# A new opening order for a chunked state-space scan and a GELU expert on one core: decay rows in one load, constants moved, half of a mask off VectorE

## The chip, the cores and the metric

The kernel runs on one core of a Trainium2 chip. The metric is the device time of one execution in microseconds, as the median of several runs. A core has TensorE (PE, with its weight loads PEld), VectorE (DVE), ScalarE (ACT), GpSimd (POOL) and SyncE (SP), which here only issues transfers; ACT's queue issues a few as well.

## The reference

Two stages, computed in one kernel. The first is a chunked linear recurrence over 4 batches, 8 heads, 768 positions, with 32 values and 16 state entries for each head:

```
log_a = log(clip(a, 1e-6, 1))
for each chunk c:
    cum  = cumsum(log_a of the chunk)
    L    = exp(cum_i - cum_j), lower triangle only
    y    = ((C B^T) * L) x  +  (C state) * exp(cum)
    state = exp(sum of log_a) * state + sum_j B_j x_j exp(cum_last - cum_j)
```

The second takes y as 3072 tokens of 256 values: `out = gelu_tanh(y @ w_in) @ w_out` with w_in of 256x2048 and w_out of 2048x256. Everything comes and goes in float32; the kernel works in bfloat16 inside.

## The kernel before

The 768 positions of a batch are cut into 6 chunks of 128; two chunks of a batch are a unit u (0 to 11), so a unit is 256 tokens. Units 0 to 2 belong to batch 0, 3 to 5 to batch 1, and so on. The work is a list of named steps, made by `add(engine, function, ...)`. The order in which they are issued, and so the order on every engine and every queue, is written out by hand in the string `ORDERED` (L19 to L72). `name.u.i:E` is a step with its arguments and, where there is a choice, its engine (A for ACT, D for DVE, P for POOL, S for SP). `~n` is a fill: matmuls of zeros on PE over n times 128 columns, written to a bank that nobody reads (L693). A step waits only for what it depends on, but each engine takes its own steps strictly in this order.

The steps that matter here:

- The decay of batch 0's first four chunks. `load_aq` brings the rows (four loads of 16 KB, L158), `clipq` clips them, `Rq` scans them (products from the end of a chunk), `tpq` turns them to positions on partitions, `recip0` takes the reciprocal (L335 to L348). `peq`, `ppq` and `pendq` make the decay of a whole chunk for each head: a small product on DVE, a matmul with the selection matrix `selp` on PE, a copy (L350 to L360). The decay of all other chunks goes the same way through `load_a`, `clip`, `R`, `tp2`, `tp6`, `recip1`, `recip`, `pe`, `pp`, `pend`.
- `mulb` and `mulc` scale B and C by decay and inverse decay, `tw` turns them on PE, `ew` copies the turned blocks out of PSUM (L408 to L431).
- `G.u` multiplies B and C of a unit into banks ga and gb (L591). `M.u.0` and `M.u.1` (DVE, L604) mask ga and gb with the triangle `tri`. For unit 0 the second half goes another way: `GE` copies a bank of gb out on ACT (L609), and `ME` masks the copy on POOL by a select, or on DVE by a product (L612).
- x of the first four chunks is loaded in one piece of 512 KB (`load_x4`), cast in two halves of its heads (`x4.0`, `x4.1`, L551), and brought into chunk order on PE by `XX.u` with the matrix `unp` that `c_unp` builds (L256); `xn` copies it out. `XD.u` is the state's new part.
- `S.c` carries the state on (DVE), `SP.c` spreads it by head under `bmask` for the next chunk (L681). `Y.u` sums the masked part and the state's part (L634), `yev.u` copies it to `xm`, the expert's input.
- The expert: `s1.u.i` (i = 0 to 7) is four matmuls into one of two banks hp (L700), `gelu.u.i` takes the bank to bfloat16 on ACT (L712), `s2.c.q` is four matmuls that add a quarter of the second product of chunk c (L717), `oev.c` copies the sum out and `store.c` stores it.
- The weights come as four pieces of w_in (`load_wi.q`) and four of w_out (`load_wo.q`), 512 KB each, and are cast in halves (`wi.q.k`, `wo.q.k`). `s1.u.i` needs piece i/2 (rounded down) of w_in, `s2.c.q` needs piece q of w_out.
- Constants: `c_ident`, `c_tri`, `c_bmask`, `c_m8`, `c_cz` are made on POOL, `c_zero`, `c_m4`, `c_sel` (a reduction, and the copy that makes `selp`), `c_par`, `c_unp` on DVE. `c_warm` runs the GELU once on one value.

Of the kernel before, what the change touches and what calls it, by code (L numbers as in the profile page):

```python
# [17 lines left out]
SCR = (2, 3)  # L18
ORDERED = """  # L19
# [8 lines left out]
gelu.0.3 load_bc.1.0 s1.0.4 wi.3.0:A s1.0.5 gelu.0.4 Y.1 tp2 mul1.0 gelu.0.5 yev.1.0.2:A s1.0.6  # L28
s1.0.7 gelu.0.6 load_x.2 tp6.0 load_bc.1.1 load_x.3 gelu.0.7 recip1 T1.0 s2.0.1.0.o s1.1.0 bh1:D N1
s1.1.1 wo.1.1:A tp6.3 s2.0.0.1.o wo.2.1:P gelu.1.0 gelu.1.1 mul1.1 tp6.2 T1.1 tp6.1 ce1.1:A ce1.0:A  # L30
wo.2.0:A bn1:D recip.1.4 s2.0.1.1.o s1.1.2 s1.1.3 gelu.1.2 wo.3.0:A wo.3.1:P G.2 gelu.1.3 s2.0.0.2.o
s2.0.1.2.o s2.0.0.3.o castx.2.None:P s2.0.1.3.o load_bc.2.1 M.2.0 mul.1.0 M.2.1 oev.1:A s1.1.4
s1.1.5 T.1.0 load_x.4 oev.0:A s2.1.0.0.o castx.3.None:P s2.1.0.1.o gelu.1.4 SP.3 D.2 gelu.1.5 s1.1.6
S.2.0 SP.4 load_x.5 E.1.0:A N.1 mul.1.1 bn.1:D gelu.1.6 s1.1.7 Y.2 s2.1.0.2.o T.1.1 gelu.1.7
yev.2.0.2:A s1.2.0 s1.2.1 gelu.2.0 E.1.1:D F.1 s2.1.0.3.o s1.2.2 gelu.2.1 gelu.2.2 D.3 load_bc.2.0
oev.2:D G.3 S.3.0 S.3.1 s2.1.1.0.o load_x.6 castx.4.None:P s1.2.3 gelu.2.3 s2.1.1.1.o s2.1.1.2.o
# [51 lines left out]
def kernel(  # L88
# [53 lines left out]
    def a_rows(t, n):  # L142
        return bass.AP(tensor=a.tensor, offset=a.offset + t, ap=[[S, batch * H], [1, n]])
# [112 lines left out]
    def c_unp():  # L256
# [3 lines left out]
        for r in range(R4):  # L260
            nc.vector.tensor_copy(out=unp[:, r, :, r], in_=sub)
# [701 lines left out]
```

## Time and profile before

| | |
|---|---|
| device time, median of 2 runs | 117.23 us (117.01 to 117.46) |
| span of the profiled execution | 115.1 us |
| its granted TensorE clock | 1.000 |
| PE busy | 109.4 us (95%) |
| ACT busy | 75.1 us (65%) |
| DVE busy | 68.7 us (60%) |
| POOL busy | 15.1 us (13%) |

The page gives for the profiled execution the span from its first to its last instruction, and no other time of its own; the device times of the two runs also hold what lies around that span. PE's busy time counts the fills, and its ends are modelled. Busy shares are averages: the first 14 us, the next 15 and the rest have different limits, and are read apart. A row of the timeline has the start and the busy time in us, then the engine and the line; where like instructions are merged (x2, x14) the busy time is that of all of them.

### The profile page before, as it was taken

What the parts mean: (1) busy time and instruction counts of PE and PEld (TensorE: products, weight loads), DVE (VectorE), ACT (ScalarE), POOL (GpSimd) and SP (SyncE); (2) the same over time, 40 slices, a digit from 0 to 9 for tenths busy, and PEclk for the clock granted to TensorE, in tenths of its full rate; (3) what the DMA queues carried; (4) which work ended last, traced back from release to release, by engine and by line L of the source; (5) the groups of instructions that cost most, each with busy time, mean ns of one, the idle gap of its engine ahead of it and who ended that gap; (6) DMA issues with size and microseconds to landing.
All of it is one profiled execution on the core that took longest, in us unless ns stands there. A gap on an engine that the chain in (4) does not pass through costs nothing.

```text
span 115.1 us, 3372 instructions
## 1 busy us (share of the span) xinstructions
PE 109.4 (95%) x1425; PEld 92.2 (80%) x1425; DVE 68.7 (60%) x135; ACT 75.1 (65%) x149; POOL 15.1 (13%) x32
## 2 busy tenths in 40 slices
PE   6999799999999999999999999999999999999990
PEld 2354578978877979799898998998989989999970
DVE  6688799998799989196966281546827421000100
ACT  3119889978657767657576486377766765685710
POOL 6564274122220000020002000000000000000000
PEclk9999999999999999999999999999999999999999
DMA  2999999949969828959478760000014014001132
GB/s 65 236 280 286 397 293 311 278 84 218 225 109 226 214 64 203 192 147 265 102 158 184 174 178 0 6 0 0 0 50 138 0 49 139 0 0 51 46 103 79
DMA packets 43006, 15.97 MB, mean 139 GB/s; under 512 B 36656, under 2 KB 41456, under 8 KB 42992
## 3 DMA queue, kind: packets, MB, share of 16 engines
q1 hardware_dynamic: 42848, 15.68, 53.9%
q8 instruction: 11, 0.18, 0.6%
q10 hardware_dynamic: 144, 0.08, 0.4%
q14 instruction: 3, 0.02, 0.1%
HBM read 11.04 MB, written 3.93 MB: 130 GB/s over the span
## 4 chain that ended last, share of the span: by engine, by line
PE 82%; DMA 8%; SPq 4%; POOL 1%; issue 1%; ACT 0%
PE hp L709 36%; PE o_ps L727 33%; DMA wf<-in_moe_w_out_dram 8%; PE yb L727 3%; PE ga L595 3%; PE yb L650 2%; PE yb L659 2%; SPq L190 1%; PE hp L628 1%; SPq L162 1%; SPq L159 1%; SPq L150 1%; POOL w_out_sb L316 1%; POOL w_in_sb L316 1%; SPq L183 1%
## 5 line engine op out<-in xcount | busy, mean ns | idle before, releaser
L713 ACT ACTIVATE gT<-hp 128x512 bf16<-128x512 f32 x96 | 53.3, 595 | 24.5 <-PE hp L709 24.0
L709 PE MATMUL hp<-xm,w_in_sb 128*128 128x256 bf16 x384 | 51.9, 273 | 0.5 <-ACT pend L314 0.3
L727 PE MATMUL o_ps<-w_out_sb,gT 128*128 128x256 bf16 x352 | 46.4, 273 | 0.0
L709 PEld LDWEIGHTS <-w_in_sb 128*128 128x128 bf16 x384 | 41.2, 114 | 3.2 <-issue 1.7
L727 PEld LDWEIGHTS <-gT 128*128 128x128 bf16 x384 | 37.0, 98 | 4.7 <-issue 0.8
L318 DVE COPY o_sb<-o_ps 128x256 f32<-128x256 f32 x7 | 3.0, 424 | 22.4 <-PE o_ps L727 18.4
L605 DVE TENSOR_TENSOR m<-ga,tri 128x1024 bf16<-128x1024 f32 x12 | 14.6, 1216 | 0.0
L605 DVE TENSOR_TENSOR m<-gb,tri 128x1024 bf16<-128x1024 f32 x11 | 13.4, 1219 | 0.5 <-PE gb L595 0.5
L697 PE MATMUL yb<-wz 128*128 128x512 bf16 (+2 forms) x24 | 8.2, 491 | 1.1 <-DVE warm L222 1.1
L314 ACT ACTIVATE o_sb<-o_ps 128x256 f32<-128x256 f32 x15 | 5.6, 382 | 4.1 <-PE o_ps L727 3.0
L683 DVE SCALAR_TENSOR_TENSOR sp_new<-s_new,pend,bmask 128x256 bf16<-128x256 f32 x17 | 8.0, 479 | 0.1
L316 POOL CAST x<-x_t 128x512 bf16<-128x512 f32 x5 | 3.2, 648 | 34.9 <-DMA x_t<-in_x_dram 22.9
L676 DVE SCALAR_TENSOR_TENSOR s_new<-s_new,pend,hp 128x64 f32<-128x64 f32 x13 | 3.6, 279 | 5.7 <-PE hp L628 5.5
L697 PEld LDWEIGHTS <-wz 128*128 128x128 bf16 x25 | 2.9, 126 | 5.0 <-issue 3.6
L659 PE MATMUL yb<-m,x 128*32 128x128 bf16 x192 | 6.1, 219 | 0.0
L650 PE MATMUL yb<-ce,sp_new 128*32 128x128 bf16 x160 | 5.3, 220 | 0.0
L595 PE MATMUL ga<-ce,bh 32*128 32x256 bf16 x48 | 4.7, 272 | 0.1
L314 ACT ACTIVATE xm<-yb 128x512 bf16<-128x512 f32 x8 | 4.8, 597 | 0.0
L595 PE MATMUL gb<-ce,bh 32*128 32x256 bf16 x48 | 4.7, 273 | 0.0
L727 PE MATMUL yb<-w_out_sb,gT 128*128 128x256 bf16 x32 | 4.1, 273 | 0.0
L659 PEld LDWEIGHTS <-x 128*32 128x32 bf16 x192 | 3.8, 97 | 0.4 <-issue 0.2
L650 PEld LDWEIGHTS <-sp_new 128*32 128x32 bf16 x160 | 3.0, 96 | 1.0 <-issue 1.0
(108 smaller groups left out, 78.4 us busy)
## 6 DMA issues: line engine op xcount, KB each, us to landing
out_dram<-o_sb SPq DMA_DIRECT2D x24, 128.0 KB, 2.0
x_t<-in_x_dram SPq DMA_DIRECT2D x20, 128.0 KB, 3.8
wf<-in_moe_w_in_dram SPq DMA_DIRECT2D x4, 512.0 KB, 8.3
wf<-in_moe_w_out_dram SPq DMA_DIRECT2D x4, 512.0 KB, 8.9
bc_t<-in_B_dram SPq DMA_DIRECT2D x3, 384.0 KB, 4.8
bc_t<-in_C_dram SPq DMA_DIRECT2D x3, 384.0 KB, 4.3
scr<-bc SPq DMA_DIRECT2D x4, 192.0 KB, 3.1
x_t<-in_x_dram SPq DMA_DIRECT2D x1, 512.0 KB, 4.8
```

The costliest lines, as they stand in the source:

```text
L314: nc.scalar.activation(o, i, AF.Copy)
L316: nc.gpsimd.tensor_copy(out=o, in_=i)
L595: nc.tensor.matmul(out=gbank(g)[:, 256 * k:256 * k + 256], lhsT=bh_of(2 * u + k)[gs], rhs=ce_of(2 * u + k)[gs], start=True, stop=True, til ...
L605: nc.vector.tensor_tensor(out=m_of(u)[:, 2 * i:2 * i + 2].rearrange("p g k e t -> p (g k e) t"), in0=gx[i].rearrange("p g (k t) -> p (g k) ...
L650: nc.tensor.matmul(out=y4[32 * j:32 * j + 32, k, w], lhsT=sp[:, 32 * h:32 * h + 32], rhs=ce_of(gc)[:, h % 2], start=first(j), stop=False, ...
L659: nc.tensor.matmul(out=y4[32 * j:32 * j + 32, k, w], lhsT=X16[u][:, k, 32 * h:32 * h + 32], rhs=m[:, h // 2, h % 2, :], start=first(j), st ...
L676: nc.vector.scalar_tensor_tensor(out=s_new, in0=state[("s", gc - 1)], scalar=pend_of(gc), in1=d, op0=ALU.mult, op1=ALU.add)
L683: nc.vector.scalar_tensor_tensor(out=sp_new.rearrange("p (g d) -> p g d", g=4), in0=(XN[0][:, H * D:H * D + 64] if gc == 0 else state[("s" ...
L697: nc.tensor.matmul(out=t[:, 0:m * 128], lhsT=wz, rhs=w3.to_broadcast([128, m, 128]), start=True, stop=True, skip_group_check=True)
L709: nc.tensor.matmul(out=hp[:, j * T:(j + 1) * T], lhsT=w_in_k[:, w, q, k], rhs=xm[:, w, u * T:(u + 1) * T], start=(w == 0), stop=(w == 1))
L713: nc.scalar.activation(gts[u][:, 2 * i:2 * i + 2], hps.pop((u, i)).rearrange("p (j t) -> p j t", j=2), AF.Gelu_apprx_tanh)
L727: nc.tensor.matmul(out=ops[gc], lhsT=gts[u][:, fi, k * Q:(k + 1) * Q], rhs=w_out_sb[:, fi, :], start=(fi == 0 and (u > 0 or k == 0)), stop ...
```

## The change

- `load_aq` is one load of 128 rows of 512 B on ACT's queue (the rows that are not used hold shifted decays), in place of four on two queues.
- `c_unp` becomes two steps: the zeros on POOL (`c_unp0`), and one copy with four diagonals in place of four copies. `c_m4` moves ahead of `c_zero`; `c_bmask`, `c_cz`, `c_tri` come right behind `c_ident`; `c_par` and `c_sel` stand between `tpq` and `peq`; `c_m8` comes much later.
- x of the first four chunks is loaded and cast by unit: `x4.u.k` handles 64 partitions, so `XX.0` needs only the first half of the partitions. That makes four casts.
- Unit 1's gb goes the way of unit 0's: `GE.1.2` and `GE.1.3` on ACT, `ME.1.2` on POOL, `ME.1.3` on DVE (it has a buffer of its own).
- `SP.c` may run on POOL for every chunk but the first, as two instructions with a float32 tile between them. The new order does so for chunks 1, 2, 3, 6, 7 and 10; the others stay on DVE.
- `load_bc0` brings B ahead of C; `load_wo.0` comes right behind `load_wi.0`; B of the last two chunks of batch 0 and of batch 1 come ahead of `load_wi.2`, C of batch 1 ahead of `load_wi.3`.
- A first s1 step no longer waits for the last one of the unit before (unit 1 only), and the whole order is new: units 0 and 1 go through the expert in turns, unit 3 is handled ahead of unit 2.

```diff
-c_wz c_ident c_zero c_unp load_aq.2:A load_bc0.1 c_tri load_aq.1:S load_aq.3:S load_aq.0:A c_m8
-c_sel c_warm c_m4 load_bc0.0 load_x4 clipq Rq tpq load_a.0:A load_a.1:S peq ~53 ppq pendq:A
-load_wi.0 c_cz c_bmask recip0 mulc.0:D mulc.1:D mulb:P ~9 tw.1 tw.0 ew.0.0:D c_par ew.0.1:A tw.2
-ew.0.2:A x4.1:D ~8 G.0 clip ew.1.0:A ew.1.1:A load_wi.1 M.0.0 GE.3 x4.0:P GE.2 load_wi.2 ~2 XX.0
-XD.0 load_wo.0 xn.0:A ew.1.2:A SP.0 S.0.0 xn.1:A wi.0.0:A wi.0.1:A R ~13 G.1 S.0.1 load_wi.3 XX.1
-load_bc1.0 xn.2:A ME.3:P ME.2:P pe Y.0 XD.1 pp yev.0.0.2:A S.1.0 load_wo.1 load_bc1.1 SP.1 S.1.1
-load_wo.2 wi.1.1:P M.1.0 wi.2.0:P wo.0.0:D pend:A wo.0.1:P wi.2.1:P SP.2 wi.1.0:A M.1.1 s1.0.0
-gelu.0.0 s1.0.1 gelu.0.1 xn.3:A wi.3.1:P s1.0.2+4 gelu.0.2 s1.0.3 s2.0.0.0.o load_wo.3 wo.1.0:P
...
+c_wz load_aq:A load_bc0.0 load_bc0.1 c_ident c_cz c_bmask c_tri c_m4 c_zero clipq Rq tpq c_par c_sel
+peq mulb:P c_unp0 load_x4.0 load_x4.1 load_wi.0 ~33 ppq recip0 pendq:D tw.0 mulc.0:D c_warm ew.0.0:A
+load_a.0:A load_a.1:A load_wo.0 load_wi.1 mulc.1:P x4.0.0:P x4.0.1:P ~8 tw.1 ew.0.1:A tw.2 c_unp
+ew.1.0:D ew.0.2:A x4.1.1:P x4.1.0:D ~15 G.0 ew.1.1:A ew.1.2:A GE.0.3 M.0.0 XX.0 GE.0.2 ME.0.3:P XD.0
+xn.0:A xn.1:A S.0.0 ME.0.2:P ~4 G.1 SP.0 S.0.1 ~3 Y.0 XX.1 M.1.0 SP.1:P XD.1 wi.0.1:D load_bc1.0
+load_bc.1.0 load_wi.2 load_bc1.1 S.1.0 wi.0.0:P GE.1.3 GE.1.2 ME.1.2:P yev.0.0.2:A xn.2:A xn.3:A
+SP.2:P s1.0.0 ME.1.3:D Y.1 gelu.0.0 s1.0.1 c_m8 wo.0.0:P wi.1.0:P wo.0.1:P wi.1.1:P yev.1.0.2:A
+gelu.0.1 s1.1.0 s1.1.1 gelu.1.0 gelu.1.1 S.1.1 clip R pe tp2 mul1.0 tp6.3 tp6.0 recip1 tp6.1 tp6.2
+s2.0.0.0.o mul1.1 load_wo.1 pp s1.1.2 pend:A load_bc.1.1 s1.1.3 T1.0 s2.0.1.0.o gelu.1.2 load_wi.3
+gelu.1.3 s1.0.2 load_wo.2 bh1:A gelu.0.2 load_wo.3 load_x.3 mul.1.0 s1.0.3 gelu.0.3 wi.2.1:P
+wi.2.0:P N1 T1.1 s1.1.4 bn1:A s1.0.4 gelu.1.4 wo.1.1:P wo.1.0:P wi.3.0:P T.1.0 gelu.0.4 s1.0.5
+load_x.2 ce1.0:A recip.1.4 ce1.1:D s1.1.5 gelu.0.5 mul.1.1 s2.0.0.1.o gelu.1.5 E.1.0:D T.1.1
+s2.0.1.1.o E.1.1:A wi.3.1:D N.1 bn.1:A F.1 wo.2.1:P s1.0.6 s1.0.7 wo.2.0:D gelu.0.6 G.3 s2.0.0.2.o
+gelu.0.7 M.3.1 M.3.0 wo.3.1:A s2.0.1.2.o s1.1.6 load_x.4 gelu.1.6 wo.3.0:P s2.0.0.3.o s2.0.1.3.o
+s1.1.7 castx.3.None:P oev.0:A oev.1:D load_x.5 load_x.7 load_bc.2.1 D.3 S.3.0 SP.6:P castx.2.None:P
+SP.3:P gelu.1.7 G.2 s2.1.0.0.o s2.1.0.1.o s2.1.0.2.o M.2.0 M.2.1 s2.1.0.3.o D.2 Y.3 oev.2:A
...
-    def load_aq(i, eng):
-        (nc.scalar if eng == "ACT" else nc.sync).dma_start(out=aq_t[32 * i:32 * i + 32], in_=a_rows(i * Q, Q))
+    def load_aq(eng):
+        (nc.scalar if eng == "ACT" else nc.sync).dma_start(
+            out=aq_t, in_=bass.AP(tensor=a.tensor, offset=a.offset, ap=[[P4, 16], [S, H], [1, Q]]))
...
-    def load_x4():
-        nc.sync.dma_start(out=x4_t, in_=x[0, :, 0:R4 * Q, :].rearrange("h (p r) d -> p h (r d)", r=R4))
+    def load_x4(u):
+        nc.sync.dma_start(out=x4_t[64 * u:64 * u + 64], in_=x[0, :, u * T:(u + 1) * T, :]
+                          .rearrange("h (p r) d -> p h (r d)", r=R4))
...
-        nc.vector.memset(unp, 0.0)
+    def c_unp0():
+        nc.gpsimd.memset(unp, 0.0)
...
-        for r in range(R4):
-            nc.vector.tensor_copy(out=unp[:, r, :, r], in_=sub)
+        d = unp[:, 0, :, 0]
+        diag = bass.AP(tensor=d.tensor, offset=d.offset, ap=[list(d.ap[0]), [Q + 1, R4], [R4, P4]])
+        nc.vector.tensor_copy(out=diag, in_=sub.rearrange("p (o q) -> p o q", o=1).to_broadcast([128, R4, P4]))
...
-    def f_GE(g):
-        nc.scalar.activation(ge0[:, g - 2], gbank(g), AF.Copy)
+    def f_GE(u, g):
+        nc.scalar.activation(ge0[GEU.index(u)][:, g - 2], gbank(g), AF.Copy)
...
+        if eng == "POOL":
+            sc = spf[gc % 2]
+            nc.gpsimd.tensor_scalar(out=sc, in0=state[("s", gc)], scalar1=pend_of(gc + 1), scalar2=None, op0=ALU.mult)
+            nc.gpsimd.tensor_tensor(out=sp_new.rearrange("p (g d) -> p g d", g=4),
+                                    in0=sc.rearrange("p (o d) -> p o d", o=1).to_broadcast([128, 4, 64]),
+                                    in1=bmask.rearrange("p (g d) -> p g d", g=4), op=ALU.mult)
...
-        if u:
+        if u not in GEU:
...
-                s.deps.append(s1.get((u - 1, NI - 1)))
+                s.deps.append(s1.get((u - 1, NI - 1)) if u > 1 else None)
```

More of the change, by code (lines that the diff above doesn't have):

```diff
@@ L31 @@
[L31 to L36, printed above, removed]
@@ L72 @@
+s1.11.2 oev.20:A s1.11.3 store.20 gelu.11.2 s2.10.1.0.o store.18 gelu.11.3 s2.10.1.1.o s1.11.4
+s1.11.5 gelu.11.4 s2.10.1.2.o gelu.11.5 s2.11.0.0.yb s1.11.6 s1.11.7 gelu.11.6 s2.10.1.3.o gelu.11.7
+s2.11.0.1.yb oev.21:D s2.11.0.2.yb store.21 s2.11.0.3.yb s2.11.1.0.o oev.22:A s2.11.1.1.o store.22
+s2.11.1.2.o store.19 s2.11.1.3.o oev.23:A store.23
 """
@@ L156, in load_bc1 @@
                           .rearrange("h (p r) n -> p h (r n)", r=n))
-    def load_aq(i, eng):
-        (nc.scalar if eng == "ACT" else nc.sync).dma_start(out=aq_t[32 * i:32 * i + 32], in_=a_rows(i * Q, Q))
+    def load_aq(eng):
+        (nc.scalar if eng == "ACT" else nc.sync).dma_start(
+            out=aq_t, in_=bass.AP(tensor=a.tensor, offset=a.offset, ap=[[P4, 16], [S, H], [1, Q]]))
     def load_a(i, eng):
-        (nc.scalar if eng == "ACT" else nc.sync).dma_start(out=a_t[32 * i:32 * i + 32], in_=a_rows(i * HS, HS))
+        (nc.scalar if eng == "ACT" else nc.sync).dma_start(out=a_t[32 * i:32 * i + 32], in_=a_rows(i, HS))
     def load_bc(b, i):
@@ L297 @@
     xm = const.tile([128, 2, n_tokens], BF16, name="xm")
+    spf = [const.tile([128, 64], FP32, name=f"spf{i}") for i in range(2)]
     gx = [ps1.tile([128, 2, 512], FP32, name=f"g{i}") for i in "ab"]
@@ L549, with f_x4 @@
     XN = {}
[L551 to L553 removed]
+    def f_x4(u, k, eng):
+        ps, ks = slice(64 * u, 64 * u + 64), slice(4 * k, 4 * k + 4)
+        copy(eng, x4b[ps, ks].rearrange("p h r d -> p h (r d)"), x4_t[ps, ks])
     def f_XX(u):
@@ L679, in f_S, with f_SP @@
         state[("s", gc)] = s_new
-    def f_SP(gc):
+    def f_SP(gc, eng):
         sp_new = st.tile([128, 256], BF16, name="sp_new")
+        if eng == "POOL":
[4 more added lines that the diff above has]
+                                    in1=bmask.rearrange("p (g d) -> p g d", g=4), op=ALU.mult)
+            state[("sp", gc)] = sp_new
+            return
         nc.vector.scalar_tensor_tensor(
@@ L772 @@
     add("A", c_warm, deps=[cz0])
-    cunp = add("D", c_unp, deps=[cid])
+    cu0 = add("P", c_unp0)
+    cunp = add("D", c_unp, deps=[cid, cu0])
     cpar = add("D", c_par, deps=[cbm])
```

101 lines of the change are left out of this document (47 added, 54 removed).

## The prediction, made before the changed kernel had run

> **What bounds the kernel now.** I read the page first, then the table of four stretches, then the timeline of the opening and of the stretch behind it, then the chain and the transfers issue by issue.
>
> ```profile
> span 115.1 us, 3372 instructions
> ...
> PE   6999799999999999999999999999999999999990
> ...
> DMA  2999999949969828959478760000014014001132
> GB/s 65 236 280 286 397 293 311 278 84 218 225 109 226 214 64 203 192 147 265 102 158 184 174 178 0 6 0 0 0 50 138 0 49 139 0 0 51 46 103 79
> ...
> PE 82%; DMA 8%; SPq 4%; POOL 1%; issue 1%; ACT 0%
> ```
> ```profile
> 0.00:14.18 14.18, 12.01 (x161) 5.89 (x162) 10.48 (x36) 7.13 (x18) 7.27 (x20) 1.00 0.86 252
> 14.18:29.00 14.82, 14.32 (x167) 12.23 (x166) 14.16 (x27) 13.28 (x27) 5.24 (x8) 1.00 0.92 236
> 29.00:107.70 78.70, 78.70 (x1062) 70.30 (x1061) 43.65 (x73) 52.85 (x102) 2.62 (x4) 1.00 0.46 106
> ```
>
> The second table gives, behind each stretch, its length and the busy time of PE, PEld, DVE, ACT and POOL, the granted clock, the DMA share and GB/s. From 29 us on TensorE never stops, in either order of the same work, so I cost that stretch at nothing: what can move the time lies before it. Up to 14.18 PE's busy time is mostly fill matmuls, and between 14.18 and 29 DVE and ACT are nearly full too and the transfers run at 0.92. The question is thus when the first expert matmul (s1.0.0) starts and how tightly PE works until weights and units are all there.
>
> ```profile
> 0.80 0.91 ACTq L159 DMA_DIRECT2D aq_t<-in_a_dram  x2
> ...
> 1.05 5.76 PE L697 MATMUL yb<-wz 128*128 128x512 bf16 x14 [1.05 <-DVE warm L222]
> ...
> 1.75 0.28 DVE L258 TENSOR_REDUCE sub<-ident 128x32 bf16<-128x128 bf16 x1
> ...
> 3.67 0.45 POOL L238 TENSOR_SCALAR_AFFINE_SELECT bmask<-bmask 128x256 bf16<-128x256 bf16 x1
> 3.70 0.50 DVE L273 COPY selp<-sel 128x128 f32<-128x128 f32 x1
> ...
> 5.16 0.23 DVE L328 TENSOR_SCALAR acq<-aq_t 128x128 f32<-128x128 f32 x1 [0.89 <-DMA aq_t<-in_a_dram]
> ...
> 5.88 0.40 DVE L342 STREAM_TRANSPOSE rt<-rq_t 128x128 f32<-128x128 f32 x1
> ...
> 6.21 0.25 DVE L351 TENSOR_SCALAR peq<-m,acq,rq_t 128x4 f32<-128x4 f32 x1
> ...
> 6.37 1.05 POOL L416 TENSOR_TENSOR bc0s<-bcf,rt 128x512 bf16<-128x512 f32 x1 [1.74 <-DVE rt L342]
> ...
> 6.80 1.24 DVE L409 TENSOR_TENSOR cz<-bcf,pt 128x256 bf16<-128x256 f32 x2
> 6.85 0.65 PE L697 MATMUL yb<-wz 128*128 128x512 bf16 x3
> 7.03 0.17 ACT L314 ACTIVATE pendq<-hp 128x4 f32<-128x4 f32 x1 [3.79 <-PE hp L356]
> ...
> 8.76 0.21 DVE L266 TENSOR_REDUCE par<-bmask 128x1 f32<-128x4 bf16 x2
> ...
> 9.08 0.28 PE L595 MATMUL ga<-ce,bh 32*128 32x256 bf16 x2
> ...
> 9.51 1.23 DVE L605 TENSOR_TENSOR m<-ga,tri 128x1024 bf16<-128x1024 f32 x1
> ...
> 10.22 1.22 POOL L616 TENSOR_SCALAR_AFFINE_SELECT m<-ge 128x512 bf16<-128x512 bf16 x2 [1.71 <-ACT ge L610]
> ...
> 11.07 0.48 DVE L683 SCALAR_TENSOR_TENSOR sp_new<-o_ps,pendq,bmask 128x256 bf16<-128x256 f32 x1 [0.33 <-ACT x L314]
> 11.47 0.21 DVE L674 COPY s_new<-o_ps 128x64 f32<-128x64 f32 x1
> ...
> 13.16 0.61 POOL L316 CAST w_in_sb<-wf 128x512 bf16<-128x512 f32 x1 [1.72 <-DMA wf<-in_moe_w_in_dram]
> ...
> 14.18 1.03 PE L709 MATMUL hp<-xm,w_in_sb 128*128 128x256 bf16 x8 [0.28 <-ACT pend L314]
> ...
> 14.39 0.28 DVE L676 SCALAR_TENSOR_TENSOR s_new<-s_new,pendq,o_ps 128x64 f32<-128x64 f32 x1
> ```
>
> Times are the start and the busy time. The old opening is a chain: the decay rows land (5.16), clip, scan and turn end at 6.28, peq ends at 6.46, the scaled B and C are turned on PE, G.0 starts at 9.08, and s1.0.0 at 14.18. Two things in these rows decide my sum. First, DVE and POOL get in each other's way: the copy of selp took 0.50 us beside a POOL select that ran until 4.12, and two products of 256 elements (L409) took 1.24 where the first one lay under POOL's product until 7.42. Second, the fills: 14 of 512 columns in 5.76 us are 0.43 us apart up to 6.57; the three after 6.85 take 0.65 together, so TensorE then runs at twice the rate, although the granted clock is 1.00 all along.
>
> **The change, part by part.** *Decay rows in one load.* Four loads of 16 KB become one of 64 KB, first on ACT's queue at 0.80, and SP's queue no longer carries two of them and one of a_t before the weights.
>
> ```profile
> aq_t<-in_a_dram ACTq DMA_DIRECT2D x1, 16.0 KB, 2.0
> ```
> ```profile
> bcf<-in_C_dram SPq DMA_DIRECT2D x1, 256.0 KB, 3.1
> ```
>
> Both were issued at 0.80; they bound the landing: 2.8 to 3.9. I take 3.3. Clip to turn lasted 1.12 (5.16 to 6.28), so tpq ends at 4.5; POOL's selects of 0.45 for bmask and tri now run beside it, which I put at 0.1 (0 to 0.6). 4.6, against 6.28.
>
> *Early constants moved.* c_par and c_sel now stand on DVE between tpq and peq, and GpSimd starts mulb as soon as tpq ends: 4.7 to 5.75. c_par takes 0.21 and c_sel's reduction some 0.28 (the row of sub), so the copy of selp comes at about 5.1, in the middle of mulb. By the selp row I let it wait until 5.75; with 0.2 for the copy and 0.25 for peq, peq ends at 6.2. Behind the waiting copy stand peq, recip0, pendq and mulc.0 on DVE; ppq on PE and mulc.1 on POOL wait for them. Without the wait it would be 5.55; the ends are 5.05 (landing 2.8, no wait) and 7.25 (landing 3.9, 0.6 behind selects, wait). So of 1.7 us gained at tpq, 0.26 is left at peq. The Trainium skill ("SBUF — State Buffer", Who interferes with whom) goes further than the selp row: not copies alone but tensor_scalar operations too take the port pair that GpSimd works through, exclusively and for a whole instruction. By that rule clipq would as a rule wait out one of POOL's selects, which no row here shows; the sum would then be 118.8 instead of the 118.4 below.
>
> *From peq to G.0* the old kernel took 2.62 (6.46 to 9.08). In the new order PE does ppq (0.39, from 6.46 to 6.85), tw.0, 8 units of fill, tw.1, tw.2, 15 units, G.0; a unit is 128 columns, 0.107 at the slow rate and 0.054 at the fast. POOL's mulc.1 comes first (half of mulb's elements: 0.53, at most 1.05), mulc.0 after it, about when PE gets to tw.1. At the fast rate this is 2.7 and the data decide; at the slow rate throughout 4.4. Which? The old fills ran 5.5 us without a break before the rate doubled. The new ones are 33 units, 3.5 us, and end at 4.57; then PE idles until 6.3. That is nearest to the slow state, so I take it up to tw.2 and the fast one for the 15 units: 0.5 + 0.43 + 0.85 + 0.86 + 0.81 + 0.1 = 3.55. G.0 at 9.75 (7.75 to 11.65), where it was 9.08.
>
> *From G.0 to s1.0.0* (old: 5.10). New, on DVE: mask M.0.0 from +0.43 for 1.23, S.0.0 0.21, SP.0 0.48, S.0.1 0.28, M.1.0 1.22: +3.85. POOL has two masks of 0.61 for pair 0, then SP.1 (a product of 256 elements, 0.53 to 1.05, and a small one before it, 0.2), then the cast wi.0.0 (0.61), ending at +4.0 to +4.5; the cast wi.0.1 on DVE comes behind it, 0.43. s1.0.0 at +4.7 (4.3 to 5.2), so 14.45. The half load of x costs two more casts of 0.6 on POOL, under the fills; c_unp0, the split of c_unp and c_m8 (moved behind SP.2) lie on POOL and DVE while PE waits for others, each under 0.5 us.
>
> *From s1.0.0 to s1.1.7.*
>
> ```profile
> 15.67 1.03 PE L709 MATMUL hp<-xm,w_in_sb 128*128 128x256 bf16 x8
> ...
> 17.51 0.96 PE L709 MATMUL hp<-xm,w_in_sb 128*128 128x256 bf16 x7 [0.25 <-POOL w_in_sb L316]
> ...
> 23.39 0.59 ACT L713 ACTIVATE gT<-hp 128x512 bf16<-128x512 f32 x1
> ...
> 23.90 0.61 POOL L316 CAST w_out_sb<-wf 128x512 bf16<-128x512 f32 x1 [0.67 <-DMA wf<-in_moe_w_out_dram]
> ...
> 28.55 0.60 PE L709 MATMUL hp<-xm,w_in_sb 128*128 128x256 bf16 x4
> ...
> 30.09 0.50 PE L484 MATMUL gb<-ident,bc 128*128 128x128 bf16 x6
> ```
> ```profile
> 22.54 0.87 PE hp L709 x8
> ```
>
> Eight expert matmuls take 0.87 in the chain, so a step of four is 0.44. s1.1.7 (28.55 and four matmuls) ends at 28.99 in the old order. At that step the old order has issued two s2 steps and D.2 (0.97) that the new one has not, and the new one T.1.1 (0.33): the old kernel's equal point is 28.35, that is 14.17 after s1.0.0, with 1.2 us lost in gaps (0.62 before 15.67, 0.42 before 17.51, and small ones). The new order has 12.8 us of PE work here: 16 s1 and 8 s2 steps 10.5, Y.1 0.55, three sets of six transposes 1.0, G.3, pp and the small turns 0.75. Its losses I work out at 2.25. Y.1 stands right behind s1.0.0 and waits for SP.2 on POOL, which comes behind wi.0.0 and ME.1.2 (+4.0 to +5.75): 0.75 lost, and s1.0.1 and all the rest of PE queue behind it. Then s1.0.2 to s1.1.5 are six s1 steps with no s2 between them: a gelu is 0.59 for 0.44 of PE, 0.9 lost, and bh1, bn1 and ce1.0 on ACT take 1.1 more while PE has only 0.5 of turns: 0.6. So 15.05 (14.2 to 15.9): the new point is 14.45 + 15.05 = 29.5, 1.15 later than 28.35.
>
> *Loads reordered.* B and C of batch 1, 786 kB together, now stand ahead of w_in's last and w_out's last two pieces. At the page's 236 to 397 GB/s that is 2.0 to 3.3 us. The last piece was there at 23.87; with 0.3 won at the start it comes at 25.6 to 26.9, and after a cast (0.63), two s2 steps and one s1 step the point is at 27.5 to 28.8. In my sum that is hidden, since the forecast's point is 29.5; it is a floor for everything faster. load_a goes out on ACT behind ew.0.0, lands by 12, and is used after 15.
>
> *Steady order, GpSimd's later SP steps.* SP.6, SP.3, SP.7, SP.10 at 0.75 to 1.25 instead of 0.48 feed Y steps that stand 2 us of PE work behind: nothing (0 to 0.2).
>
> The sum: 115.1 + 1.15 = 116.25 of span. What lies around the span is 2.13 (the two runs' median 117.23 less 115.1; the page gives no other time for that execution), so **118.4 us**.
>
> **The rivals.** (1) *The early start pays*: the selp copy is not held up and TensorE is fast by 6: peq 5.55, G.0 8.25, s1.0.0 12.85, and with 14.6 behind it 27.45, with the loads at 397 GB/s just in time. 0.9 earlier: 116.4. For it: tpq surely ends well over a microsecond sooner. Against: the 0.50 of selp and the 1.24 of L409. (2) *The loads set the end*: the chain is early but the last w_out piece is not: 28.8, 117.7. For it: DMA share 0.92 in that stretch. Against: the chain is later still by my sum. (3) *TensorE stays slow*, the case on the slower side: one mechanism, the break in the fills at 4.57. If the doubled rate does not come before about 10.5, G.0 is at 10.6 and XX, XD, G.1 and Y.0 (0.6 more) make s1.0.0 15.9: 1.45 later than the forecast's, 119.8. For it: 5.5 us of unbroken fills in the old trace before the rate changed; against: fills and turns after 6.3 are dense again. The Trainium skill ("TensorE: Matmul & The Clock Gate", What's actually happening) has the gate opening after a busy window of about 3.4 us that runs freely, not from the kernel's start; by that rule 3.5 us of fills suffice only if a window happens to lie on them, and it would give this rival's time in most executions. The old trace, with 5.5 us, fits the rule. (4) *The change does nothing that shows*: gains and losses cancel, 117.2.
>
> **How the numbers follow.** Forecast 0.50 (117.6 to 119.2), rival 1 0.14, rival 2 0.13, rival 3 0.17, rival 4 0.06. Two per cent, 2.3 us, is about what a measurement of this kernel can tell from no change. Faster by that needs under 114.9, below rival 1's floor of loads: 0.04. Slower means over 119.6: most of rival 3 and little of the forecast, 0.13. Range 116.2 to 120.0: it takes in rival 1's floor and rival 3's price. The sum's own ends are wider (peq and the rate alone span 3.9 us at G.0), but they need all costs at one end.
>
> **What would show it.** Right: the first clip on DVE near 3.4; selp's copy ending only when mulb does; peq near 6.2; G.0 later than 9.08; a PE gap between s1.0.0 and Y.1 with SP.2 on POOL as releaser; s1.1.7 ending near 29.5, and PE full behind it. Wrong: G.0 before 8.5, or s1.0.0 before 13, or gaps of PE with a weight transfer as releaser, or new PE gaps behind 30.

## The result, and the profile after

The changed kernel takes **127.53 us** (median of 2 runs, 127.03 to 128.02), the kernel before 117.23: a ratio of 1.0874, 95% interval 1.0762 to 1.0985. The forecast was 118.4, at most 120.0. The profiled execution took 128.02 us with a span of 126.3; the other had a span of 125.3. A ratio compares only the executions that lie within 1.5% of the fastest of their kernel.

The page of the changed kernel, first the span, the busy row and granted clock of its 40 slices, then the chain that ended last and one of the costliest groups:

```profile
span 126.3 us, 3370 instructions
...
PE   6559938389799999999999999999999999999990
...
PEclk9999995868999999999999999999999999999998
...
PE 76%; DVE 8%; POOL 5%; ACT 4%; DMA 3%; issue 1%; POOLq 0%
...
L395 DVE TENSOR_TENSOR pe<-pe,m 64x24 f32<-64x24 f32 x1 | 5.6, 5597 | 0.6 <-POOL m L256 0.6
```

In the old page PE was full from the sixth slice on, the granted clock was full throughout, and DVE was not in the chain at all. Now PE has holes up to the eleventh slice, the clock falls to 0.5 in one of them, and one DVE instruction, a product of 64x24 elements whose like took 0.18 us before, takes 5.6 us and lies in the chain. The table of stretches (length, busy time of PE, PEld, DVE, ACT and POOL, granted clock, DMA share, GB/s), cut at the start of s1.0.0 and at the end of s1.1.7, says where the time went:

```profile
0.00:16.92 16.92, 11.69 (x152) 5.64 (x152) 9.80 (x30) 6.71 (x16) 10.41 (x24) 1.00 0.93 237
16.92:39.15 22.23, 17.56 (x162) 13.46 (x162) 19.66 (x28) 12.73 (x26) 9.61 (x18) 0.85 0.76 188
39.15:126.30 87.15, 83.77 (x1106) 74.69 (x1104) 42.62 (x71) 54.07 (x104) 7.54 (x12) 0.99 0.39 89
```

The old stretches, with the equal point at 28.35, were 14.18, 14.17 and 86.75. So of the 11.2 us that the span of the profiled execution grew, 2.74 lie before s1.0.0, 8.06 between s1.0.0 and s1.1.7, and 0.4 behind.

**Before s1.0.0**, from the timeline of DVE, POOL and PE (start, busy time, engine, line, and in brackets the idle time before with its releaser):

```profile
4.78 0.23 DVE L336 TENSOR_SCALAR acq<-aq_t 128x128 f32<-128x128 f32 x1 [2.64 <-DMA aq_t<-in_a_dram]
...
6.32 1.25 DVE L280 COPY selp<-sel 128x128 f32<-128x128 f32 x1
7.04 0.55 DVE L359 TENSOR_SCALAR peq<-m,acq,rq_t 128x4 f32<-128x4 f32 x1
```
```profile
5.98 1.05 POOL L424 TENSOR_TENSOR bc0s<-bcf,rt 128x512 bf16<-128x512 f32 x1 [1.93 <-DVE rt L350]
6.98 0.53 POOL L233 MEMSET unp<- 128x512 bf16 x1
```
```profile
8.47 1.06 PE L713 MATMUL yb<-wz 128*128 128x512 bf16 x2
9.32 1.06 PE L433 MATMUL hp<-ident,cz 128*128 128x128 bf16 x8
10.18 1.81 PE L713 MATMUL yb<-wz 128*128 128x512 bf16 x4
11.92 0.40 PE L603 MATMUL ga<-ce,bh 32*128 32x256 bf16 x2
```

The decay rows are there at 4.78, 0.38 earlier than before. The copy of selp then lies under two POOL instructions in turn, mulb and the zeros of c_unp0, which end at 7.51; the copy ends at 7.57 and peq at 7.59, where it had ended at 6.46. The fills are 0.43 apart, the slow rate, so that G.0 comes at 11.92 instead of 9.08.

**Behind s1.0.0**, DVE and POOL:

```profile
18.87 0.45 DVE L393 TENSOR_TENSOR pe<-ac,r_t 64x3 f32<-64x3 f32 x1
19.89 5.60 DVE L395 TENSOR_TENSOR pe<-pe,m 64x24 f32<-64x24 f32 x1 [0.58 <-POOL m L256]
```
```profile
19.82 0.60 POOL L324 CAST w_out_sb<-wf 128x512 bf16<-128x512 f32 x1
20.38 0.61 POOL L324 CAST w_in_sb<-wf 128x512 bf16<-128x512 f32 x1
20.93 0.61 POOL L324 CAST w_out_sb<-wf 128x512 bf16<-128x512 f32 x1
21.49 1.73 POOL L324 CAST w_in_sb<-wf 128x512 bf16<-128x512 f32 x3
23.17 1.17 POOL L324 CAST w_out_sb<-wf 128x512 bf16<-128x512 f32 x2
24.29 0.61 POOL L324 CAST w_in_sb<-wf 128x512 bf16<-128x512 f32 x1
24.85 1.34 POOL L324 CAST w_out_sb<-wf 128x512 bf16<-128x512 f32 x2
```

The casts are 0.56 apart and 0.61 long, so each begins before the last one has ended, and the product of pe lies under ten of them. It ends at 25.49, about where the tenth does. The last two casts together take 1.34, where two in a row took 1.17, so there is a short break between them. In the kernel before, the same product ran while POOL was idle:

```profile
12.82 0.18 DVE L387 TENSOR_TENSOR pe<-pe,m 64x24 f32<-64x24 f32 x1
```

The PE side, and the table of stretches with the granted clock:

```profile
16.92 0.63 PE L725 MATMUL hp<-xm,w_in_sb 128*128 128x256 bf16 x4 [1.06 <-POOL w_in_sb L324]
19.36 0.40 PE L658 MATMUL yb<-ce,sp_new 128*32 128x128 bf16 x8 [1.42 <-POOL m L253]
19.90 2.75 PE L725 MATMUL hp<-xm,w_in_sb 128*128 128x256 bf16 x12
25.64 0.37 PE L401 MATMUL hp<-pe,selp 64*128 64x24 f32 x2 [2.40 <-DVE pe L395]
25.94 1.67 PE L725 MATMUL hp<-xm,w_in_sb 128*128 128x256 bf16 x8
38.71 0.60 PE L725 MATMUL hp<-xm,w_in_sb 128*128 128x256 bf16 x4
```
```profile
18.00:19.00 1.00, 0.00 (x0) 0.00 (x0) 0.97 (x2) 0.18 (x1) 0.92 (x2) 1.00 1.06 310
19.00:20.00 1.00, 0.64 (x17) 0.45 (x18) 0.42 (x2) 0.00 (x0) 0.86 (x5) 0.71 1.08 361
20.00:22.00 2.00, 2.00 (x10) 1.33 (x11) 2.00 (x1) 1.36 (x3) 2.00 (x4) 0.50 0.96 342
...
27.00:29.00 2.00, 2.00 (x12) 1.51 (x11) 1.94 (x5) 1.26 (x3) 0.44 (x1) 0.50 1.04 166
```

Two losses show at once, beside the waits in brackets at s1.0.0 and in Y.1: pp waits 2.40 us for pe, and twelve expert matmuls take 2.75 us, where eight took about 1.04 before, at a granted clock of 0.50. Which of the two costs the time, or whether one brings the other, the trace alone does not say.

### The profile page after: what moved, and what is told of

The parts are those of the page before. It is cut to its first block, busy times and chain, and to the rows that moved or that the text cites. A ratio compares the mean times of both kernels' runs of the same rounds, so it can differ in the third digit from the quotient of the medians.

```text
span 126.3 us, 3370 instructions
## 1 busy us (share of the span) xinstructions
PE 113.0 (90%) x1417; PEld 93.8 (74%) x1417; DVE 72.1 (57%) x128; ACT 73.5 (58%) x143; POOL 27.6 (22%) x53
## 4 chain that ended last, share of the span: by engine, by line
PE 76%; DVE 8%; POOL 5%; ACT 4%; DMA 3%; issue 1%; POOLq 0%
PE hp L725 32%; PE o_ps L743 29%; DVE pe L395 4%; DMA aq_t<-in_a_dram 3%; PE yb L743 3%; PE ga L603 3%; ACT gT L729 2%; PE yb L713 2%; PE yb L658 2%; PE yb L667 2%; POOL sp_new L694 1%; POOL spf L693 1%; DVE selp L280 1%; ACT ge L618 1%; PE hp L636 1%
## 5 line engine op out<-in xcount | busy, mean ns | idle before, releaser
L725 PE MATMUL hp<-xm,w_in_sb 128*128 128x256 bf16 x384 | 54.0, 282 | 1.1 <-POOL w_in_sb L324 1.1
L743 PE MATMUL o_ps<-w_out_sb,gT 128*128 128x256 bf16 x352 | 47.3, 275 | 0.0
L725 PEld LDWEIGHTS <-w_in_sb 128*128 128x128 bf16 x384 | 42.2, 116 | 4.6 <-issue 1.3
L326 DVE COPY o_sb<-o_ps 128x256 f32<-128x256 f32 x9 | 3.8, 425 | 26.3 <-PE o_ps L743 23.2
L613 DVE TENSOR_TENSOR m<-gb,tri 128x1024 bf16<-128x1024 f32 x10 | 12.2, 1220 | 0.4 <-PE gb L603 0.4
L713 PE MATMUL yb<-wz 128*128 128x512 bf16 (+2 forms) x17 | 7.3, 575 | 1.0 <-DVE wz L223 1.0
L699 DVE SCALAR_TENSOR_TENSOR sp_new<-s_new,pend,bmask 128x256 bf16<-128x256 f32 x13 | 6.5, 505 | 0.2
L693 POOL TENSOR_SCALAR spf<-s_new,pend 128x64 f32<-128x64 f32 x4 | 2.4, 603 | 17.0 <-ACT gT L729 12.6
L395 DVE TENSOR_TENSOR pe<-pe,m 64x24 f32<-64x24 f32 x1 | 5.6, 5597 | 0.6 <-POOL m L256 0.6
L713 PEld LDWEIGHTS <-wz 128*128 128x128 bf16 x17 | 2.2, 140 | 3.8 <-issue 2.7
```

The source lines that it names most:

```text
L326: nc.vector.tensor_copy(out=o, in_=i)
L395: nc.vector.tensor_tensor(out=pe2, in0=pe1.rearrange("p (o c) -> p o c", o=1).to_broadcast([64, 2 * batch, HC]), in1=m8.rearrange("p (j o) ...
L613: nc.vector.tensor_tensor(out=m_of(u)[:, 2 * i:2 * i + 2].rearrange("p g k e t -> p (g k e) t"), in0=gx[i].rearrange("p g (k t) -> p (g k) ...
L699: nc.vector.scalar_tensor_tensor(out=sp_new.rearrange("p (g d) -> p g d", g=4), in0=(XN[0][:, H * D:H * D + 64] if gc == 0 else state[("s" ...
L713: nc.tensor.matmul(out=t[:, 0:m * 128], lhsT=wz, rhs=w3.to_broadcast([128, m, 128]), start=True, stop=True, skip_group_check=True)
L725: nc.tensor.matmul(out=hp[:, j * T:(j + 1) * T], lhsT=w_in_k[:, w, q, k], rhs=xm[:, w, u * T:(u + 1) * T], start=(w == 0), stop=(w == 1))
```

## The experiments

Three theories were written down. A: VectorE's small product is shut out behind GpSimd's casts, and TensorE waits for it. B: TensorE's halved clock, after breaks in its work, costs the time. C: the late opening chain does. Spans are compared below where a kernel was run once, and against the changed kernel's profiled 126.3. Single spans move: the changed kernel's other execution had 125.3, and the kernel before had 117.2 in its one run beside the first four (118.88 us), where its profiled execution had 115.1. So a difference of a microsecond between single runs shows nothing. Beside the next four runs the kernel before took 117.18 us (12 runs), beside the last three 117.21 (17 runs).

**e1_pe_gpsimd.**

```diff
-        nc.vector.tensor_tensor(
+        nc.gpsimd.tensor_tensor(
             out=pe2, in0=pe1...
-... s1.0.1 c_m8 wo.0.0:P ... gelu.1.1 S.1.1 clip R pe tp2
+... s1.0.1 c_m8 S.1.1 clip R pe wo.0.0:P ... gelu.1.1 tp2
```

> The changed kernel, with the small product in pe (64x24, the one that took 5.60 us on VectorE) done by GpSimd ahead of the ten weight casts; nothing else differs. Theory A (VectorE's product is shut out as long as GpSimd's casts follow each other without a break, and pp, pend and all that stands behind it on VectorE wait): the product is done by 20.5 instead of 25.5, TensorE's idle 2.4 us before pp goes, tp2, T1 and what follows come some 5 us earlier, 122 to 124 us. Theory B (TensorE's halved clock from 19 to 29 us is the main cost): only the 2.4 us of idle goes, 125 us. Theory C (the opening chain, 2.7 us late at the first expert matmul, is the main cost): 126 to 127 us.

Measured: 124.93 us, span 123.2. pe took 0.22 us on POOL and pp no longer waits, but the next DVE product of two SBUF operands was shut out in its place, by the same casts (from 19.07 to 24.13):

```profile
19.32 5.09 DVE L443 TENSOR_TENSOR bc0s<-bcf,rt 128x256 bf16<-128x256 f32 x1
```

So it is not this instruction but whichever product of this kind comes when the casts run. The time by itself is the one that theory B named (125); of what theory A named, the early product came and the early followers did not.

**e2_more_fills.**

```diff
-load_wi.0 ~33 ppq ... SP.2:P s1.0.0 ME.1.3:D Y.1
+load_wi.0 ~60 ppq ... SP.2:P ~16 s1.0.0 ME.1.3:D ~24 Y.1
```

> The changed kernel with more fills on TensorE: 60 units instead of 33 before ppq, 16 units before s1.0.0 and 24 before Y.1, so that it has no long idle stretch up to 19 us. Theory B (halved clock): the clock is full from about 6.6 on and stays so, G.0 comes 1 us earlier, the expert matmuls of 20 to 29 us run at full rate, 121 to 123 us. Theory A: the product on VectorE is still shut out until the casts end, TensorE then waits longer for pp, 125 to 127 us. Theory C: 126 us, by the earlier G.0 alone.

Measured: 123.09 us, span 121.4, granted clock 1.0 throughout; G.0 at 9.74, s1.0.0 at 14.52, s1.1.7 ends at 34.27. The longer fills, and the full rate with them, are worth 4.9 us of span (3.9 against the changed kernel's other execution). pp still waits 1.34 for pe:

```profile
17.50 3.35 DVE L395 TENSOR_TENSOR pe<-pe,m 64x24 f32<-64x24 f32 x1 [0.57 <-POOL m L256]
```

**e3_sel_early.**

```diff
-c_m4 c_zero clipq Rq tpq c_par c_sel peq ... mulc.0:D c_warm
+c_m4 c_sel c_zero clipq Rq tpq peq ... mulc.0:D c_par c_warm
```

> The changed kernel with c_sel on VectorE before c_zero, while the decay rows are still on their way, and c_par behind mulc.0: the copy of selp no longer runs beside GpSimd's product. Theory C: peq ends at about 6.2 instead of 7.6, G.0 at 10.5 instead of 11.9, and all later steps follow: 126 us. Theories A and B: the 1.4 us are taken back at Y.1 or at pp, 127 to 127.5 us.

Measured: 127.33 us, span 125.6. peq ends at 5.91 instead of 7.59, yet PE runs at half rate, G.0 comes at 10.78, and what is left of the gain is lost behind s1.0.0: the first product of pe (64x3) now meets the casts, 4.43 us, and pp waits 2.76. The span is lower by 0.7, less than the two executions of the changed kernel differ by, so no gain is shown for theory C.

```profile
19.22 4.43 DVE L393 TENSOR_TENSOR pe<-ac,r_t 64x3 f32<-64x3 f32 x1
```

The opening moves by itself as much. In e1_pe_gpsimd, e4_sp_vector and e5_casts_away, which leave it up to G.0 as the change has it, G.0 came at 10.72, 11.69 and 10.51 instead of 11.92. In e5_casts_away the turns of 7.50 and the two fills behind them ran at the fast rate, in the changed kernel at the slow one.

**e4_sp_vector.**

```diff
-SP.1:P ... SP.2:P ... SP.6:P ... (all SP steps on GpSimd)
+SP.1:D ... SP.2:D ... SP.6:D ...
```

> The changed kernel with all SP steps on VectorE, as before the change. TensorE's wait of 1.4 us inside Y.1 for SP.2 on GpSimd goes. If that wait sets the pace: 126 us. Theory A: GpSimd's casts begin a microsecond and a half earlier and shut pe's product out from the same place on, so the time moves by less than 1 us unless the product gets in ahead of them. Theory B: less idle before 19 us keeps the clock up, 124 us.

Measured: 127.57 us, span 125.4. GpSimd is free sooner, starts its casts at 16.50, and now SP.2 on DVE, with two SBUF operands as well, is the one shut out:

```profile
16.72 4.56 DVE L699 SCALAR_TENSOR_TENSOR sp_new<-s_new,pendq,bmask 128x256 bf16<-128x256 f32 x1
```

Y.1 waits 4.22 for the mask behind it, and no difference in time is shown.

**e5_casts_away.**

```diff
-c_m8 wo.0.0:P wi.1.0:P wo.0.1:P wi.1.1:P yev.1.0.2:A
+c_m8 wo.0.0:A wi.1.0:A wo.0.1:A wi.1.1:D yev.1.0.2:A
-s2.0.0.0.o mul1.1 load_wo.1 ... gelu.0.3 wi.2.1:P wi.2.0:P N1
+s2.0.0.0.o mul1.1 wi.2.1:D wi.2.0:D load_wo.1 ... gelu.0.3 N1
```

> The changed kernel with six weight casts taken off GpSimd: wo.0.0, wi.1.0, wo.0.1 to ScalarE behind gelu.0.0, wi.1.1 to VectorE ahead of S.1.1, wi.2.1 and wi.2.0 to VectorE behind mul1.1; only the later casts stay on GpSimd. Fills as in the change. Theory A (a VectorE product of two SBUF operands cannot start while GpSimd casts back to back): the 64x24 product of pe takes under 1 us instead of 5.60, pp starts near 21.5 instead of 25.64, s1.1.7 ends at 34 to 35.5 instead of 39.15, device time 122.5 to 124. Theory B (the halved TensorE clock between 19 and 29 us is what costs): the clock still falls back behind s1.0.0, since PE's order is unchanged; the time stays over 126.

Measured: 122.88 us, span 121.2; s1.1.7 ends at 34.06.

```profile
18.91 0.17 DVE L395 TENSOR_TENSOR pe<-pe,m 64x24 f32<-64x24 f32 x1
...
20.13 0.42 DVE L443 TENSOR_TENSOR bc0s<-bcf,rt 128x256 bf16<-128x256 f32 x1
```

The product takes 0.17 us instead of 5.60 and pp waits for nothing, as theory A said; pp starts at 22.17, a little later than its 21.5. Not all of the 5.1 us of span is the edit's: s1.0.0 came at 15.75 here instead of 16.92, and the edit begins behind it. From s1.0.0 to the end of s1.1.7 it is 18.31 instead of 22.23. The clock still fell, as theory B said it would, but the time did not stay over 126:

```profile
16.00:18.00 2.00, 1.48 (x28) 0.74 (x30) 1.97 (x4) 1.28 (x4) 1.84 (x5) 0.50 1.03 330
18.00:20.00 2.00, 1.94 (x23) 1.16 (x16) 1.79 (x7) 1.98 (x4) 0.80 (x2) 0.50 1.08 336
```

**e6_casts_fills**: the edits of e2_more_fills and e5_casts_away together.

> The casts moved as in the run e5_casts_away, and the longer fills of the run e2_more_fills (60 units ahead of ppq, 16 ahead of s1.0.0, 24 ahead of Y.1). If shut-out product and halved clock are separate losses that add up: s1.0.0 at 14.5 as in e2_more_fills, s1.1.7 ends at 30 to 31.5, 118.5 to 120.5. If they are one and the same loss seen twice: no better than the better of the two, 122 to 123.

Measured: 120.78 us, span 119.1, s1.0.0 at 14.51, s1.1.7 ends at 31.96. Just above the range for losses that add up. The four spans:

| | casts on GpSimd | casts moved |
|---|---|---|
| fills of the change | 126.3 | 121.2 |
| longer fills | 121.4 | 119.1 |

Either cure alone gives about 5 us, both 7.2: the two losses overlap by 2.8 (5.1 + 4.9 less 7.2). These are single runs, and the opening moves in them. The stretch from s1.0.0 to the end of s1.1.7 leaves the opening out: 22.23, 18.31 with the casts moved, 19.75 with longer fills, 17.45 with both. That is 3.9 and 2.5 alone and 4.8 together, an overlap of 1.6. Why they overlap shows in part. With the longer fills the product was held for 3.35 instead of 5.60; why it got in sooner is not shown. Without the shut-out PE has no break of 2.40, and the granted clock, 0.50 in the changed kernel from 27 to 29, is 1.00 in e5_casts_away from 24 to 34.

**e7_casts_fills_sel**: e6_casts_fills with the edit of e3_sel_early.

> e6_casts_fills with the selection matrix made early on VectorE (c_sel ahead of c_zero, c_par behind mulc.0), so that its copy meets no product of GpSimd. With TensorE now at its full rate, the 1.7 us that peq comes earlier should reach G.0: G.0 at 8.5 to 9.2, s1.0.0 at 13 to 14, s1.1.7 at 29 to 30.5, 117 to 119.5. If the clock is again the limit (no full rate before G.0) nothing is gained over e6_casts_fills.

Measured: 120.46 us (4 runs), ratio to before 1.0281, interval 1.0235 to 1.0328. A miss: G.0 came at 9.66, not at 8.5 to 9.2. peq ended at 5.95, but ppq started at 6.93, behind 60 units of fill; the fills that hold the clock up had become the wait.

**e8_before_few_fills**: the kernel before with fewer fills.

```diff
-peq ~53 ppq
+peq ~33 ppq
```

> The kernel before with one number changed: 33 units of fill ahead of ppq instead of 53, as many as the changed kernel has. The theory that the break in the fills keeps TensorE at half rate (rival 3 of the prediction): the fills end near 4.6, matmuls after 6.5 stay at 0.107 us for 128 columns until past 10, G.0 at 9.8 to 10.5 instead of 9.08, s1.0.0 0.8 to 1.8 later, 118 to 119.5 where the kernel before has 117.2 to 118.9 on these chips. If fills before 5 us do not matter: within 0.3 us of the kernel before.

Measured: ratio 1.0041, interval 0.9991 to 1.0090, so on this measure no difference is shown. But its ten times lie between 116.96 and 121.84, with a median of 118.32, and the twelve of the kernel before between 116.80 and 118.55, with a median of 117.18. The profiled execution took 119.31 and shows the slow rate well behind 10 us, G.0 at 10.30 and s1.0.0 at 17.08:

```profile
12.48 1.57 PE L697 MATMUL yb<-wz 128*128 128x512 bf16 x4
17.08 1.03 PE L709 MATMUL hp<-xm,w_in_sb 128*128 128x256 bf16 x8 [0.28 <-ACT pend L314]
```

A short run of fills thus can leave TensorE slow, in a share of the executions only. The Trainium skill ("TensorE: Matmul & The Clock Gate", What's actually happening) says that the activity window runs freely and does not begin with the kernel, so that the moment of opening varies from run to run; the spread of these times agrees, though no run here moved the window by itself. So do the fills: the same 60 units, from 1.04 on, took 5.88 us in e2_more_fills, 5.47 in e6_casts_fills and 6.05 in e7_casts_fills_sel.

**e9_sp12_fills50**: e7_casts_fills_sel with two further edits.

```diff
-load_wi.0 ~60 ppq ... SP.1:P ... SP.2:P
+load_wi.0 ~50 ppq ... SP.1:D ... SP.2:D
```

> e7_casts_fills_sel with 50 units of fill ahead of ppq instead of 60, and SP.1 and SP.2 on VectorE instead of GpSimd. In e7_casts_fills_sel, ppq stood behind fills until 6.93 although peq had ended at 5.95, and SP.2 ended on GpSimd at 16.5, which Y.1 needs. If these two are what is left of the loss: G.0 at 8.8 to 9.2 instead of 9.66, s1.0.0 near 13.2 instead of 14.49, s1.1.7 ends near 30 instead of 31.98, 118.3 to 119.3. If the gelus and loads behind s1.0.0 set the end anyway: no change from 120.5.

Measured: 120.00 us (4 runs), ratio 1.0234, interval 1.0178 to 1.0291. s1.0.0 came at 13.70 and s1.1.7 ended at 30.71: some six tenths of the gains expected at both points, and 0.46 us less than e7_casts_fills_sel instead of 1.2 to 2.2.

```profile
13.70 0.60 PE L725 MATMUL hp<-xm,w_in_sb 128*128 128x256 bf16 x4
14.13 1.46 PE L713 MATMUL yb<-wz 128*128 128x512 bf16 x6
16.09 0.63 PE L725 MATMUL hp<-xm,w_in_sb 128*128 128x256 bf16 x4
17.07 1.08 PE L725 MATMUL hp<-xm,w_in_sb 128*128 128x256 bf16 x8 [0.36 <-ACT xm L322]
...
21.87 1.06 PE L725 MATMUL hp<-xm,w_in_sb 128*128 128x256 bf16 x8 [0.30 <-DVE w_in_sb L326]
...
25.47 0.51 PE L492 MATMUL gb<-ident,bc 128*128 128x128 bf16 x6 [0.77 <-DVE bc L483]
```

Its own fills hold PE from 14.13 until past 15.4, although the last mask for Y.1 ends at 14.66; then come the smaller waits in brackets. The new order needs fills to stay fast and pays for them.

**e10_before_one_load**: the kernel before with one part of the change.

```diff
-c_unp load_aq.2:A load_bc0.1 c_tri load_aq.1:S load_aq.3:S load_aq.0:A c_m8
+c_unp load_aq:A load_bc0.1 c_tri c_m8
-peq ~53 ppq
+peq ~47 ppq
```

(`load_aq` is the changed kernel's single load.)

> The kernel before with one part of the change alone: the decay rows in one load of 64 KB, and, so that ppq does not stand behind fills, 47 units of fill instead of 53. If the part is worth what its landing gives (clip at 4.5 instead of 5.16, the rest of the chain as before): G.0 at 8.4 to 8.6 instead of 9.08, s1.0.0 0.3 to 0.6 earlier or held by the cast of w_in at 13.16 to 13.8, 116.6 to 117.2 where the kernel before has 117.2. If TensorE loses its full rate by the six missing units: slower by 0.5 to 3.

Measured: 116.66 us (12 runs), ratio 0.9944, interval 0.9915 to 0.9974. The new load and the six fills fewer were not run apart; with all 53 units ppq would probably have waited for the fills, which hold PE until 6.66 in the kernel before. The clip starts at 4.39 instead of 5.16, G.0 at 8.39 instead of 9.08, s1.0.0 at 13.53 instead of 14.18, and the clock holds:

```profile
5.83 0.39 PE L357 MATMUL hp<-peq,selp 128*128 128x4 f32 x2
6.08 0.65 PE L698 MATMUL yb<-wz 128*128 128x512 bf16 x3
```

This version is faster than both kernels, by a small but clear 0.55 us of the medians against the one before.

**e11_mask1_vector**: e9_sp12_fills50 with unit 1's half mask back on VectorE.

```diff
-GEU = (0, 1)
+GEU = (0,)
-GE.1.3 GE.1.2 ME.1.2:P yev.0.0.2:A ... ME.1.3:D ~24 Y.1
+yev.0.0.2:A ... M.1.1 ~24 Y.1
```

> e9_sp12_fills50 with one part of the change undone: the second half of unit 1's mask goes back to VectorE as one product out of PSUM (M.1.1, 1.22 us) instead of GE.1.2, GE.1.3, ME.1.2 and ME.1.3. If that part is what the change's authors wanted of it, VectorE's 1.22 instead of 0.63 ahead of Y.1 costs 0.3 to 0.6 us against e9_sp12_fills50; if GpSimd's select was the hindrance (it stands ahead of nothing else once SP.2 is on VectorE), there is no difference beyond 0.3.

Measured: 120.95 us (4 runs), ratio 1.0321, interval 1.0254 to 1.0388, against 1.0234 for e9_sp12_fills50: 0.95 us more by the medians, above the 0.3 to 0.6 expected. The intervals overlap, but they hold the spread of the kernel before as well; all four times here (120.58 to 121.16) lie above all four of e9_sp12_fills50 (119.88 to 120.13). So in this order that part of the change helps. Where is only in part seen: Y.1 itself was not later (s1.0.1 at 15.77), but T1.1 waits 0.54 for DVE's bc0s further on.

## Why the prediction was wrong

**The opening** was foreseen in kind and undersized in each term. *The landing* was put at the time 3.3 with a bound of 3.9, between a load of 16 KB that took 2.0 from its issue and one of 256 KB that took 3.1; but the four old loads of 16 KB took 2.0 to 3.1 themselves. The new one took 4.0 here and 3.5 to 3.8 in the other runs, and the clip stood at 4.78 here and between 4.33 and 4.64 there. *The copy of selp* waited for mulb as argued, but then for c_unp0's zeros too: 1.25 us, peq at 7.59 where 6.2 was said and 7.25 was the bound. The failing step is "c_unp0 ... while PE waits for others": its place behind mulb was not held against the copy. (No run moved these zeros alone; in e3_sel_early the copy was made early, beside two other memsets of POOL, and took 0.68.) *From peq to G.0* 3.55 was forecast, 4.33 measured, since the slow rate went on through the last 15 units and until 12.5; the end "at the slow rate throughout 4.4" was the right one for this execution. It was 4.34 in e4_sp_vector, but 3.47 in e1_pe_gpsimd and 3.31 in e5_casts_away, with the same order up to there: which rate comes when is not settled by the order. *From G.0 to s1.0.0* 4.7 was forecast, 5.0 measured. Together s1.0.0 was 2.47 later than forecast; in e1_pe_gpsimd and e5_casts_away it came at 15.87 and 15.75, 1.4 and 1.3 later. Rival 3, the break in the fills, was thus at work. The Trainium skill's rule that the prediction set beside it ("TensorE: Matmul & The Clock Gate", What's actually happening) stands with the trace here: 3.5 us of fills did not bring the full rate while they ran (9 in 3.70 us), the longer fills of e2_more_fills (15 in 5.88 us) did.

**The stretch behind s1.0.0** is where the forecast broke: 22.23 against 15.05. The step that failed is the sentence that put c_m8 and the steps near it at under 0.5 us "while PE waits for others", together with the working of losses that stood behind it. Y.1's wait for SP.2, which that working had at 0.75, was there and was 1.42. But it counted gelus, casts and copies engine by engine, and never asked what DVE does while POOL casts without a pause. The prediction had the pair's interference in hand for the opening (selp's 0.50, L409's 1.24) and priced it at one instruction of the other engine. In the new order ten casts stand in a row without a break, c_m8 releases pe at just the moment when they begin, and the price is the whole row: 5.60. Runs e1, e3 and e4 move the loss to another instruction, e5 removes it. The old kernel runs the same product at 12.82 in 0.18 us; its POOL is idle there.

The Trainium skill has the ground of this: "SBUF — State Buffer", Who interferes with whom, says that a VectorE instruction with both inputs in SBUF contends with GpSimd instructions that read SBUF. The trace agrees: the products and SP.2, with two such inputs, were held for 3.35 to 5.60 us, and in e9_sp12_fills50 two transposes, with one input, took their usual 1.05 together beside two casts:

```profile
19.62 1.05 DVE L350 STREAM_TRANSPOSE rt<-r_t 32x192 f32<-32x192 f32 x2
```
```profile
19.47 1.17 POOL L324 CAST w_out_sb<-wf 128x512 bf16<-128x512 f32 x2 [5.81 <-DMA wf<-in_moe_w_out_dram]
```

The prediction cited that section for a smaller matter, the clip, which met no select (they ended at 4.05, before it) and so showed nothing. In e10_before_one_load the clip began at 4.39 beside a select that ran from 4.18 to 4.62, and took 0.32 instead of 0.23.

**The clock** was weighed in the opening only. That it would fall again, behind s1.0.0, was no rival: PE did one expert step and half of Y.1 between 15.9 and 19.36, and the granted clock was 0.50 from 20 to 22 and from 27 to 29. Rival 3 was priced at 1.45; with this second fall, and with the casts left where they are, the longer fills win 3.9 to 4.9 in this order (e2_more_fills).

**The loads** never set the end: POOL waited on no weight transfer between 19.82 and 26.19, so the floor of rival 2 was not reached. **Behind s1.1.7** the forecast was nothing, the measurement 0.4, too little to look further. What lies around the span was taken as 2.13, the difference of two numbers from different executions; it was 1.72 in the profiled one.

What stays open: with casts moved, longer fills and SP.1 and SP.2 on VectorE (e9_sp12_fills50), 2.8 us are left against the kernel before (120.00 against 117.21). From s1.0.0 to the end of s1.1.7 it takes 17.01 instead of 14.17. The waits in its rows (1.43) and the fills held past 14.66 (0.86) lie in that stretch; they were not taken away one by one. Nor was it tried what lets the held product in. It got through at a break in the row of casts, or at its end, in the changed kernel, e1, e3 and e4, but in e2_more_fills as one cast (20.21) gave way to the next (20.76). And in the kernel before a product with two operands in SBUF ended at 16.97, with a cast on each side of it, the second of which took 0.80 instead of 0.61:

```profile
16.14 0.83 DVE L683 SCALAR_TENSOR_TENSOR sp_new<-s_new,pendq,bmask 128x256 bf16<-128x256 f32 x1
```
```profile
15.83 0.87 POOL L316 CAST w_out_sb<-wf 128x512 bf16<-128x512 f32 x1 [0.71 <-DMA wf<-in_moe_w_out_dram]
16.65 0.80 POOL L316 CAST w_in_sb<-wf 128x512 bf16<-128x512 f32 x1
```

## What to carry to other kernels

Before a row of casts goes to GpSimd, list what VectorE does in that time with two operands in SBUF: such an instruction can wait for the end of the row, not for one cast, and whatever TensorE needs from it is late by all of that. Move some of the casts to other engines (here ScalarE and VectorE), rather than move the one instruction seen waiting; the next one takes its place. Whether breaks in the row would do as well was not tried. An earlier start is worth little if TensorE then runs slow: in e3_sel_early peq ended 1.68 earlier, and no gain in time is shown. The single load, the one part of this change that was tried in the old order, helped there, in an order that kept TensorE busy.

## What the runs showed of the hardware

A 64x24 product of VectorE took 5.60 us beside GpSimd's casts and 0.17 without them; a 64x3 product took 4.43 and 0.15. The granted clock in the table of stretches stands at 1.00 in the opening of the changed kernel although its fills are 0.43 apart, twice the 0.22 of the fast rate: the rate has to be read from the spacing of like matmuls there. In e5_casts_away, where the rate had been fast from 7.5 and was slow again by 9, the same column does show it, with 0.50 from 9 to 12. One load of 64 KB in 128 rows landed 4.0 us after its issue (3.5 to 3.8 in the other runs), where the old profile has 2.0 to 3.1 for four of 16 KB.
